# Regrouping TensorE's queue in a local-attention and channel-mix kernel: the four W_k blocks of a unit together behind the gate

## The chip, the cores and the metric

The kernel runs on one core of a Trainium2 chip. What counts is the device time of one execution in microseconds (us). Engines are named as in the profile: PE is TensorE's matmul stream and PEld its weight loads, DVE is VectorE, ACT is ScalarE, POOL is GpSimd, and SP is the engine that issues all DMAs.

## The reference

A chunked local attention feeds a channel mix. The attention works for each of 4 batches and 8 heads on chunks of 32 queries. Each chunk sees 16 keys to its left, its own 32, 8 to its right, and 8 memory keys.

```python
scores = scale * np.matmul(q_c, k_full.transpose(0, 1, 3, 2))
a = np.exp(scores - np.max(scores, axis=-1, keepdims=True))
a = a / (np.sum(a, axis=-1, keepdims=True) + 1e-09)
out[:, :, c_start:c_end] = np.matmul(a, v_full)
...
xk = mu_k * x + (1.0 - mu_k) * x_prev
xr = mu_r * x + (1.0 - mu_r) * x_prev
k = np.maximum(xk @ w_k, 0.0)
v = k * k @ w_v
r = 1.0 / (1.0 + np.exp(-(xr @ w_r)))
return (r * v).astype(np.float32)
```

Here x is the attention's output with its heads side by side (4 x 768 tokens of 512 values), x_prev is x one token earlier, w_k is 512 x 1024, w_v 1024 x 512 and w_r 512 x 512.

## The kernel before, in words

The 3072 tokens are cut into 12 units of 256 tokens (two tiles of 128). For each unit TensorE runs these pieces of work, and each is one operation of a planner:

- s (L358): the scores of one unit's two tiles, 128 small products of 64 columns;
- t (L420): per tile, four transposes of the normalised weights to PSUM tile pt. DVE and ACT copy them to aTz;
- a (L437): per tile, 32 small products of 64 columns, the attention's output px. It is copied to xT (helper lines L262 on ACT, L264 on DVE);
- g (L523): the gate x @ w_r, two blocks (pr, one for each tile of 128 tokens) of 12 products of 512 columns;
- h (L535): the hidden layer x @ w_k, four blocks h0 to h3 (ph), each 24 products of 256 columns;
- v (L549): the output k*k @ w_v, four half blocks v0 to v3 (pv: v0 and v1 fill the first tile's bank, v2 and v3 the second's) of 12 products of 512 columns.

Operands of g, h and v are split in a high and a low part (xh and xl, wkh and wkl, and so on), so that each mathematical product is three on TensorE: high x high, high x low, low x high. Each product is preceded by a weight load of its own of 128 columns.

Between h and v, each hidden block goes through relu (L624 on ACT, L626 on DVE), square (L631, L633), the high part kh and the low part kl (L641). Between a and the gate stands the mix on DVE: df (L485), the two mixes of four instructions each (L493), then the high parts xh on ACT or DVE and the low parts xl (L503). The mix for the gate has index 1 in its names (xf, xh_1, xl_1), that for W_k index 0 (written over df; xh_0, xl_0). DVE multiplies each output tile with the gate (L682), and SP stores it (L685).

The order of all engines' queues is fixed when the program is built. te_order (L177 to L196) writes a sequence of TensorE's pieces. LEAD is its start, and for each later unit the loop appends the rest: h0, h1, both t of the next unit, h2, both a of the next unit, h3, v0, the s of the unit after next, v1, the two g of the next unit, v2, v3. The place in it gives each piece a due time. Plan.order (L106 to L174) then simulates the engines. A hand-written list, FIRST (L41), goes first. After it the planner picks, of all ready operations, the one that could start earliest, with due times as the second key. TensorE's operations are picked by the same rule, so their final order is mostly that of te_order. PSUM has four banks under the tag m for h, g and v blocks, handed out in turn, so each block waits until the bank that was given out four blocks earlier has been read.

Unit 0 is a special case: its h runs with the four row tiles of w_k outside and the blocks inside, as the weights arrive.

Of the kernel before, what the change touches and what calls it, by code (L numbers as in the profile page):

```python
# [16 lines left out]
P = 128  # L17
# [7 lines left out]
KT = DM // P  # L25
# [2 lines left out]
NEG = -3.0e38  # L28
TINY = 2.0**-112
LEAD = """s0 t0 t1 a0 a1 h0.0 h0.1 s1 h0.2 h0.3 g0.0 g0.1 t2 t3 a2 a3  # L30
v0.0 v0.1 v0.2 v0.3 g1.0 g1.1 s2"""
UTOK = 256
QPU = UTOK // P
QKW = NPAIR * NJ * (CHUNK + NK)
# [28 lines left out]
class Slot:  # L63
    def __init__(self, tag):
        self.tag = tag
        self.users = []


class Op:
# [3 lines left out]
    def __init__(self, name, alts, fn, deps, new, use, due, table):  # L73
        self.name = name
        self.alts = alts
        self.table = table
        self.fn, self.new, self.due = fn, list(new), due
        self.deps = [d for d in deps if d is not None]
        for s in dict.fromkeys(list(new) + list(use)):
            s.users.append(self)  # L80


class Plan:
# [22 lines left out]
    def order(self, listed):  # L106
        self.dues()
        free, ring, left, succ = {"port": 0.0}, {}, {}, {}
        state = {"table": "exp"}
        for o in self.ops:  # L110
            o.eng = o.end = None
            left[o] = len(o.deps)
            for d in o.deps:
                succ.setdefault(d, []).append(o)
        ready = [o for o in self.ops if not left[o]]
        done = []

        def place(o, only=None):
            at = list(o.deps)
            for k, s in enumerate(o.new):  # L120
                h = ring.get(s.tag, []) + [x for x in o.new[:k] if x.tag == s.tag]
                if len(h) >= self.bufs[s.tag]:
                    at += h[-self.bufs[s.tag]].users
            at = [d for d in at if d is not o]
            if any(d.end is None for d in at):
                return None
            best = None
            for eng, cost, port in o.alts:
                if only and eng != only:
                    continue  # L130
                if eng == "act" and o.table and o.table != state["table"]:
                    cost += TABLE
                t = free.get(eng, 0.7)
                for d in at:
                    t = max(t, d.end + (SELF[eng] if d.eng == eng else HOP))
                if port:
                    t = max(t, free["port"])
                key = t + cost + BIAS.get(eng, 0.0) * (len(o.alts) > 1)
                if best is None or key < best[0] - 1e-9:
                    best = (key, t, eng, cost, port)  # L140
            return best

        def put(o, p):
            _, t, eng, cost, port = p
            o.eng, o.start = eng, t
            free[eng] = t + cost
            if port:
                free["port"] = t + cost
            if eng == "act" and o.table:
                state["table"] = o.table  # L150
            o.end = t + cost + (DLAT if eng == "dma" else 0.0)
            for s in o.new:
                ring.setdefault(s.tag, []).append(s)
            ready.remove(o)
            done.append(o)
            for x in succ.get(o, ()):
                left[x] -= 1
                if not left[x]:
                    ready.append(x)

        byname = {o.name: o for o in self.ops}
        for item in listed:
            name, _, eng = item.partition("@")
            o = byname[name]
            put(o, place(o, eng))
        while ready:
            best = None
            for o in ready:
                p = place(o)
                if p is not None and (best is None or (p[1], o.due, o.seq) < best[0]):  # L170
                    best = ((p[1], o.due, o.seq), o, p)
            put(*best[1:])
        assert len(done) == len(self.ops)
        return done  # L174


def te_order():  # L177

    nu = B * S // UTOK
    seq = LEAD.split()  # L180
    seq = [tuple([x[0]] + [int(n) for n in x[1:].split(".")]) for x in seq]
    for u in range(1, nu):
        a, b = 2 * u + 2, 2 * u + 3
        g = [("g", u + 1, c) for c in range(QPU)]
        h = [("h", u, f) for f in range(FT // 2)]
        v = [("v", u, n) for n in range(FT // 2)]
        seq += h[:2] + [("t", a), ("t", b)] + h[2:3] + [("a", a), ("a", b)] + h[3:]
        seq += v[:1] + [("s", u + 2)] + v[1:2] + g + v[2:]
    last = {"s": nu, "g": nu, "t": B * NQT, "a": B * NQT}
    seq = [x for x in seq if x[1] < last.get(x[0], nu)]  # L190
    due, t = {}, 8.0
    for x in seq:
        assert x not in due
        due[x] = t
        t += PE_COST[x[0]]
    return due  # L196
# [3 lines left out]
def local_attention__then__channel_mix(  # L200
# [11 lines left out]
    nc = tc.nc  # L212
# [57 lines left out]
    units = [(b, u * UTOK) for b in range(B) for u in range(S // UTOK)]  # L270
    NU = len(units)
    due = te_order()
    chunks = [(w_r, wr_hl, k) for k in range(KT // 2)]
    chunks += [(w_k, wk_hl, k) for k in range(KT)]
# [53 lines left out]
    def wdeps(hl, ks):  # L328
        return [o for k in ks for o in wdone[id(hl[0]), k]]
# [181 lines left out]
    def channel_mix(u):  # L511
        b, t0 = units[u]

        def hilo(m):
            return T["xh", u, m], T["xl", u, m]
# [11 lines left out]
        def hidden(f, ks):  # L527
            p = T["ph", u, f]
            xh, xl = hilo(0)
            for i in range(2):  # L530
                fc = slice((2 * f + i) * P, (2 * f + i + 1) * P)
                for k in ks:
                    wh, wl = (w[k][:, fc] for w in wk_hl)
                    for n, (w, x) in enumerate(((wh, xh), (wh, xl), (wl, xh))):
                        nc.tensor.matmul(  # L535
                            p[:, i * UTOK : (i + 1) * UTOK], w, x[:, k],
                            start=(k + n == 0 and (u > 0 or i == 0)), stop=(k == KT - 1 and n == 2 and (u > 0 or i == 1)),
                        )

        def value(c, fs):  # L540
            p = T["pv", u, c]
# [19 lines left out]
        for n in range(QPU):  # L561
            def f_gate(n=n):
# [9 lines left out]
            w = wdeps(wr_hl, [n] if first else range(KT // 2))  # L572
            prev = op(
                f"g{u}.{n}", ("pe", BLOCK), f_gate, [prev] + xg + w,
                new=(gs if n == 0 else []) if first else [gs[n]], use=xgs + gs * first, due=due["g", u, n],
# [11 lines left out]
        for c in range(QPU):  # L587
# [3 lines left out]
                    new=[sgs] if c == 0 else [], use=[gs[c], sgs], due=due["g", u, QPU - 1] + BLOCK + 2,  # L591
# [7 lines left out]
        for n in range(FT // 2):  # L599
            def f_hidden(n=n):  # L600
                if first:
                    for f in range(FT // 2):
                        if n == 0:
                            bank("ph", u, f)
                        hidden(f, [n])
                else:
                    bank("ph", u, n)
                    hidden(n, range(KT))

            w = wdeps(wk_hl, [n] if first else range(KT))  # L610
            prev = op(
                f"h{u}.{n}", ("pe", BLOCK), f_hidden, [prev] + xk + w,
                new=(ms if n == 0 else []) if first else [ms[n]], use=xks + ms * first, due=due["h", u, n],
            )
            hdone.append(prev)
# [4 lines left out]
        for f in range(FT // 2):  # L620
# [22 lines left out]
            s, kf, kh, kl = ms[f], Slot("kf"), Slot(f"kh{f}"), Slot(f"kl{f}")  # L643
# [11 lines left out]
        for n in range(FT // 2):  # L655
# [13 lines left out]
            if first:  # L669
                new, use = (vs if n == 0 else []), use + vs  # L670
            else:
                new, use = ([vs[c]] if half == 0 else []), use + [vs[c]]
# [33 lines left out]
    with tc.manual_schedule():  # L706
        for o in plan.order(FIRST.split()):
            if o.eng == "pe":
                n = 0 if ("ph", 0, 0) in T else int((o.start - busy - 0.1) / (0.86 if busy else 1.72))
# [53 lines left out]
```

## Time and profile before

| | |
|---|---|
| device time, three runs | 421.63, 423.3, 423.85 us; median 423.3 us |
| profiled execution, first to last instruction | 420.3 us |
| mean granted TensorE clock | 0.996 |
| PE busy | 407.5 us (97%) |
| PEld busy | 354.2 us (84%) |
| DVE, ACT, POOL busy | 249.1, 186.6, 19.0 us |
| DMA queue of the data (q1) | 48.31 MB, 31.4% of 16 engines' span |

The profile shows one execution, and no time of its own beside its span; the three runs are 1.3 to 3.6 us longer than that span. The duration that the profile gives a single product covers its whole way through the array and overlaps its neighbours, so the rate of TensorE is read from the distance of starts. In the chain of waits a piece counts from the end of the one before it.

### The profile page before, as it was taken

The numbers are of one execution on the slowest core, as the hardware profiler recorded it, in microseconds if no ns is written. First come the engines' busy times: TensorE is split into PE (matmuls) and PEld (weight loads), VectorE is DVE, ScalarE is ACT, GpSimd is POOL, SyncE is SP. The second block draws the span as 40 slices with busy tenths as digits, with TensorE's granted clock in tenths as the row PEclk, the third lists the DMA queues.
The fourth block names the chain that finished last, engine by engine and source line by source line (L and its number), as shares of the span: only waits on it lengthen the run. The fifth ranks groups of instructions, "written<-read, shape, count | busy, mean of one in ns | idle before, by whom it ended". The sixth has DMA issues, their size and how long they took to land.

```text
span 420.3 us, 9878 instructions
## 1 busy us (share of the span) xinstructions
PE 407.5 (97%) x4450; PEld 354.2 (84%) x4450; DVE 249.1 (59%) x357; ACT 186.6 (44%) x274; POOL 19.0 (5%) x20
## 2 busy tenths in 40 slices
PE   6988999999999999999999999999999999999996
PEld 2447989878988988988988998998998998898994
DVE  3898989990394385386276277178179069165021
ACT  2376874760543453363354354255155255153250
POOL 2202000200000000000000000000000000000000
PEclk9899999999999999999999999999999999999999
DMA  8996966210073043034034034024030010000001
GB/s 321 389 413 236 400 209 246 76 50 27 25 249 105 25 143 136 27 117 161 27 102 176 27 101 176 27 101 177 25 101 28 25 51 28 25 2 27 25 2 50
DMA packets 12905, 48.93 MB, mean 116 GB/s; under 512 B 1472, under 2 KB 1600, under 8 KB 12352
## 3 DMA queue, kind: packets, MB, share of 16 engines
q1 hardware_dynamic: 12864, 48.31, 31.4%
q8 instruction: 35, 0.57, 0.6%
q14 instruction: 6, 0.05, 0.0%
HBM read 42.01 MB, written 6.29 MB: 115 GB/s over the span
## 4 chain that ended last, share of the span: by engine, by line
PE 85%; DMA 6%; DVE 5%; ACT 2%; issue 1%; SPq 0%; DVEq 0%; ACTq 0%
PE ph L535 30%; PE pv L549 30%; PE pr L523 14%; DMA qk<-in_qk_dram 6%; PE px L437 5%; PE s L358 4%; PE pt L420 2%; DVE mag L311 1%; DVE wvl L317 1%; DVE xl L503 1%; DVE df L493 0%; DVE xh L264 0%; DVE wvh L264 0%; ACT L383 0%; DVE kl L641 0%
## 5 line engine op out<-in xcount | busy, mean ns | idle before, releaser
L535 PE MATMUL ph<-xh,wkh 128*128 128x256 f32 x384 | 109.6, 285 | 0.0
L535 PE MATMUL ph<-xh,wkl 128*128 128x256 f32 x384 | 107.8, 281 | 0.0
L535 PE MATMUL ph<-xl,wkh 128*128 128x256 f32 x384 | 107.8, 281 | 0.0
L624 ACT ACTIVATE kf<-ph 128x512 f32<-128x512 f32 x46 | 27.4, 597 | 127.6 <-PE ph L535 124.6
L549 PE MATMUL pv<-wvh,kh 128*128 128x512 f32 x192 | 75.7, 394 | 0.5 <-ACT kf L624 0.5
L549 PE MATMUL pv<-wvh,kl 128*128 128x512 f32 x192 | 74.8, 390 | 0.0
L549 PE MATMUL pv<-wvl,kh 128*128 128x512 f32 x192 | 74.8, 390 | 0.0
L535 PEld LDWEIGHTS ph<-xh,wkh 128*128 128x128 f32 x384 | 72.4, 188 | 1.1
L535 PEld LDWEIGHTS ph<-xh,wkl 128*128 128x128 f32 x384 | 73.3, 191 | 0.0
L535 PEld LDWEIGHTS ph<-xl,wkh 128*128 128x128 f32 x384 | 72.1, 188 | 0.4
L641 DVE TENSOR_TENSOR kl<-kf,kh 128x512 fp32r<-128x512 f32 x48 | 32.9, 689 | 48.1 <-ACT kh L262 47.3
L682 DVE TENSOR_TENSOR o<-pv,sg 128x512 f32<-128x512 f32 x24 | 16.4, 688 | 71.8 <-PE pv L549 71.8
L549 PEld LDWEIGHTS pv<-wvh,kh 128*128 128x128 f32 x192 | 36.0, 188 | 8.4 <-ACT kf L624 0.9
L549 PEld LDWEIGHTS pv<-wvh,kl 128*128 128x128 f32 x192 | 36.0, 188 | 7.6
L549 PEld LDWEIGHTS pv<-wvl,kh 128*128 128x128 f32 x192 | 36.1, 188 | 6.8
L523 PE MATMUL pr<-wrh,xh 128*128 128x512 f32 x96 | 37.6, 392 | 0.0
L523 PE MATMUL pr<-wrh,xl 128*128 128x512 f32 x96 | 37.4, 389 | 0.0
L523 PE MATMUL pr<-wrl,xh 128*128 128x512 f32 x96 | 37.4, 389 | 0.0
L437 PEld LDWEIGHTS px<-aTz,vw 128*64 128x64 f32 x768 | 23.6, 138 | 5.2 <-issue 3.3
L631 ACT ACTIVATE kf<-kf 128x512 f32<-128x512 f32 x39 | 24.5, 632 | 7.1 <-DVE kf L626 6.0
L262 ACT CAST kh<-kf 128x512 fp32r<-128x512 f32 x38 | 23.6, 620 | 8.4 <-PE pv L549 5.4
L437 PE MATMUL px<-aTz,vw 128*64 128x64 f32 x768 | 25.5, 224 | 1.2 <-DMA vw<-in_vw_dram 1.0
(60 smaller groups left out, 481.7 us busy)
## 6 DMA issues: line engine op xcount, KB each, us to landing
qk<-in_qk_dram SPq DMA_DIRECT2D x24, 768.0 KB, 6.4
vw<-in_vw_dram SPq DMA_DIRECT2D x24, 512.0 KB, 4.6
out_dram<-o SPq DMA_DIRECT2D x24, 256.0 KB, 2.0
raw<-in_w_k_dram SPq DMA_DIRECT2D x4, 1024.0 KB, 8.9
raw<-in_w_v_dram SPq DMA_DIRECT2D x4, 1024.0 KB, 6.4
raw<-in_w_r_dram SPq DMA_DIRECT2D x2, 1024.0 KB, 7.5
id_sb<-in_ident_dram SPq DMA_DIRECT2D x1, 64.0 KB, 7.4
mu_sb<-in_mu_dram SPq DMA_DIRECT2D x1, 4.0 KB, 7.1
```

Of the source, the lines that this page charges most:

```text
L262: e.copy(dst, src)
L311: nc.vector.scalar_tensor_tensor(mi, mi, 3, word(0, U32), ALU.logical_shift_left, ALU.bitwise_or)
L358: nc.tensor.matmul(s5[CHUNK * j : CHUNK * (j + 1), h, c, r, :], q4[z, r, j, :], k4[z, r, j, :], start=True, stop=True,)
L420: nc.tensor.transpose(p[:, n * P : (n + 1) * P], e[:, n // 2, c, n % 2, :], id_sb)
L437: nc.tensor.matmul(p3[64 * h : 64 * h + 64, 2 * g : 2 * g + 2, CHUNK * j : CHUNK * j + CHUNK], v[:, g, h, j, :], a[:, h, g, j, :], start=True,
L523: nc.tensor.matmul(p, x[:, k, c * P : (c + 1) * P], w, start=(k + n == 0), stop=(k == KT - 1 and n == 2))
L535: nc.tensor.matmul(p[:, i * UTOK : (i + 1) * UTOK], w, x[:, k], start=(k + n == 0 and (u > 0 or i == 0)), stop=(k == KT - 1 and n == 2 and ...
L549: nc.tensor.matmul(p, x[:, tc_], w, start=(f + n == 0), stop=(f == FT - 1 and n == 2))
L624: e.activation(r, T["ph", u, f], AF.Relu)
L631: e.activation(q, q, AF.Square)
L641: e.tensor_sub(l, T["kf", u, f], T["kh", u, f].bitcast(F32))
L682: nc.vector.tensor_mul(o, T["pv", u, c], T["sg", u][:, c * DM : (c + 1) * DM])
```

## The change

Four things change.

1. te_order: in units 2 to 11 the four h blocks stand together, and before them stand the two gate blocks of the same unit. The small pieces come behind them: both t of the next unit and s, then v0, both a, v1, v2, v3, and the next gate. In unit 1 the order of what is left after LEAD stays as it was.
2. Plan.order: TensorE's operations are taken strictly in te_order's sequence (LEAD now names v1.0 ahead of v0.3, where the planner had put it). For the other engines the first key is no longer the earliest start alone: up to 0.4 us (of the planner's own time) is added for operations that are due late.
3. hidden: in every unit but the first, the very first product of h0 is issued as two products of 128 columns each, with the same weights, each with a weight load of its own.
4. As a result the planner deals out some of DVE's, ACT's and POOL's work differently.

```diff
-v0.0 v0.1 v0.2 v0.3 g1.0 g1.1 s2"""
+v0.0 v0.1 v0.2 v1.0 v0.3 g1.0 g1.1 s2"""
...
+        line = sorted((o for o in self.ops if o.alts[0][0] == "pe" and o.end is None), key=lambda o: o.rank, reverse=True)
         while ready:
             best = None
+            while line and line[-1].end is not None:
+                line.pop()
             for o in ready:
+                if o.alts[0][0] == "pe" and o is not line[-1]:
+                    continue
                 p = place(o)
-                if p is not None and (best is None or (p[1], o.due, o.seq) < best[0]):
-                    best = ((p[1], o.due, o.seq), o, p)
+                k = p and (p[1] + min(0.4, max(0.0, 0.05 * (o.due - p[1]))), o.due, o.seq)
+                if p is not None and (best is None or k < best[0]):
+                    best = (k, o, p)
...
-        seq += h[:2] + [("t", a), ("t", b)] + h[2:3] + [("a", a), ("a", b)] + h[3:]
-        seq += v[:1] + [("s", u + 2)] + v[1:2] + g + v[2:]
+        x = [("a", a), ("a", b)]
+        seq += h + [("t", a), ("t", b), ("s", u + 2)]
+        seq += x + g + v[1:] if u == 1 else v[:1] + x + v[1:] + g
...
-                        nc.tensor.matmul(
-                            p[:, i * UTOK : (i + 1) * UTOK], w, x[:, k],
-                            start=(k + n == 0 and (u > 0 or i == 0)), stop=(k == KT - 1 and n == 2 and (u > 0 or i == 1)),
-                        )
+                        start = k + n == 0 and (u > 0 or i == 0)
+                        stop = k == KT - 1 and n == 2 and (u > 0 or i == 1)
+                        step = P if u > 0 and f + i + k + n == 0 else UTOK
+                        for a in range(0, UTOK, step):
+                            nc.tensor.matmul(
+                                z[:, a : a + step], w, x[:, k, a : a + step], start=start and a == 0, stop=stop
+                            )
```

The places below are those of unit 4. The numbers behind a tile's name are those that the program gave it; the changed program's lines stand up to 11 further down (L535 is L547, L485 is L492, and so on). First TensorE's queue where the unit's h begins, before (ph is the hidden block, pv the output bank of the unit before):

```order
L549 MATMUL pv_1_1914<-wvl_81,kh_3_1778 128x512
L549 MATMUL pv_1_1914<-wvh_77,kl_3_1849 128x512
L535 MATMUL ph_0_1941<-xh_0_1851,wkh_66 128x256
L535 MATMUL ph_0_1941<-xl_0_1874,wkh_66 128x256
L535 MATMUL ph_0_1941<-xh_0_1851,wkl_70 128x256
L535 MATMUL ph_0_1941<-xh_0_1851,wkh_67 128x256
```

and with the change (pr is the gate of the same unit):

```order
L530 MATMUL pr_1_1931<-wrl_85,xh_1_1885 128x512
L530 MATMUL pr_1_1931<-wrh_83,xl_1_1904 128x512
L547 MATMUL ph_0_1946<-xh_0_1906,wkh_66 128x128 x2
L547 MATMUL ph_0_1946<-xl_0_1927,wkh_66 128x256
L547 MATMUL ph_0_1946<-xh_0_1906,wkl_70 128x256
L547 MATMUL ph_0_1946<-xh_0_1906,wkh_67 128x256
```

The gate now stands directly ahead of h, and the first product is two of 128 columns. Next the place where the transposes leave the h stream, before (between h1 and h2):

```order
L535 MATMUL ph_1_1969<-xl_0_1874,wkh_69 128x256
L535 MATMUL ph_1_1969<-xh_0_1851,wkl_73 128x256
L420 MATMUL pt_2001<-id_sb,e_1889 128x128 x4
L420 MATMUL pt_2008<-id_sb,e_1889 128x128 x4
L535 MATMUL ph_2_2015<-xh_0_1851,wkh_66 128x256
L535 MATMUL ph_2_2015<-xl_0_1874,wkh_66 128x256
```

and with the change (behind h3; s is the scores tile, pv the unit's own first output bank):

```order
L547 MATMUL ph_3_2037<-xl_0_1927,wkh_69 128x256
L547 MATMUL ph_3_2037<-xh_0_1906,wkl_73 128x256
L427 MATMUL pt_2069<-id_sb,e_1804 128x128 x4
L427 MATMUL pt_2076<-id_sb,e_1804 128x128 x4
L365 MATMUL s_2083<-qk_1435 32x64 x32
L365 MATMUL s_2083<-qk_1490 32x64 x32
L560 MATMUL pv_0_2151<-wvh_74,kh_0_2001 128x512
L560 MATMUL pv_0_2151<-wvl_78,kh_0_2001 128x512
```

The small pieces have left the h stream, and transposes and scores now follow each other. Last DVE's queue between the attention's output and the operands of the next gate, before:

```order
L485 TENSOR_TENSOR df_2121<-xT_2086 128x1024
L493 SCALAR_TENSOR_TENSOR xf_2123<-df_2121,mu_sb,xT_2086 128x256 x4
L264 CAST xh_1_2144<-xf_2123 128x1024
L493 SCALAR_TENSOR_TENSOR df_2121<-df_2121,mu_sb,xT_2086 128x256 x4
L641 TENSOR_TENSOR kl_3_2217<-kf_3_2141,kh_3_2146 128x512
L503 TENSOR_TENSOR xl_1_2221<-xf_2123,xh_1_2144 128x1024
L367 MEMSET s_2152 32x2x4x16
L371 TENSOR_REDUCE mx_2238<-s_2152 128x16
L503 TENSOR_TENSOR xl_0_2242<-df_2121,xh_0_2219 128x1024
L375 TENSOR_TENSOR e_2257<-s_2152,mx_2238 128x1024
```

and with the change:

```order
L382 TENSOR_TENSOR e_2173<-s_2083,mx_2167 128x1024
L271 COPY xT_2212<-px_2177 128x4x128
L271 COPY xT_2212<-px_2195 128x4x128
L492 TENSOR_TENSOR df_2232<-xT_2212 128x1024
L500 SCALAR_TENSOR_TENSOR xf_2234<-df_2232,mu_sb,xT_2212 128x256 x4
L693 TENSOR_TENSOR o_0_2252<-pv_0_2151,sg_1944 128x512
L500 SCALAR_TENSOR_TENSOR df_2232<-df_2232,mu_sb,xT_2212 128x256 x4
L510 TENSOR_TENSOR xl_1_2273<-xf_2234,xh_1_2254 128x1024
L394 TENSOR_REDUCE sum_2277<-e_2173 128x16
L395 TENSOR_SCALAR sum_2277<-sum_2277 128x16
```

The copies of px to xT have come from ACT to DVE, the score reductions have moved ahead of them, and the cast to xh_1 has gone to ACT. POOL, which normalised one unit's weights (L393) in the lead, no longer does that; DVE does it, behind the mix.

More of the change, by code (lines that the diff above doesn't have):

```diff
@@ L76, in __init__ @@
         self.table = table
-        self.fn, self.new, self.due = fn, list(new), due
+        self.fn, self.new, self.due, self.rank = fn, list(new), due, due
         self.deps = [d for d in deps if d is not None]
@@ L531, in hidden @@
                 fc = slice((2 * f + i) * P, (2 * f + i + 1) * P)
+                z = p[:, i * UTOK : (i + 1) * UTOK]
                 for k in ks:
```

## The prediction

> **What bounds the kernel now.** I read the page first. TensorE is busy almost throughout, at full clock nearly everywhere.
>
> ```profile
> PE 407.5 (97%) x4450; PEld 354.2 (84%) x4450; DVE 249.1 (59%) x357; ACT 186.6 (44%) x274; POOL 19.0 (5%) x20
> PEclk9899999999999999999999999999999999999999
> ```
>
> As many weight loads as products: each product has its own. Next the list of waits says who kept PE idle.
>
> ```profile
> PE s L358 <- DMA qk<-in_qk_dram: 4.5, 3, 2.7
> PE s L358 <- issue: 1.7, 1, 1.7
> PE px L437 <- DMA vw<-in_vw_dram: 1.0, 1, 1.0
> PE pv L549 <- ACT kf L624: 0.5, 1, 0.5
> ```
>
> The first three lie in the lead, where this change moves nothing on TensorE. The fourth is at 85 us. The chain of waits (start, duration) then shows where the time goes.
>
> ```profile
> 38.70 11.10 PE ph L535 x96
> ...
> 80.94 2.85 DVE mag L311
> 83.79 0.02 issue
> 83.81 1.05 ACT wvh L262
> 84.86 0.50 ACT kf L624
> 85.36 0.04 issue
> 85.41 5.73 PE pv L549 x24
> 91.14 5.44 PE pr L523 x24
> ...
> 137.09 5.66 PE ph L535 x48
> 142.75 0.87 PE pt L420 x8
> 143.62 2.83 PE ph L535 x24
> 146.45 2.02 PE px L437 x64
> 148.46 3.02 PE ph L535 x24
> 151.49 2.72 PE pv L549 x12
> 154.21 1.41 PE s L358 x89
> 155.62 2.95 PE pv L549 x12
> 158.57 5.44 PE pr L523 x24
> 164.01 5.44 PE pv L549 x24
> ...
> 394.28 11.31 PE ph L535 x96
> ```
>
> From 85.41 us to the end the chain is TensorE alone, one unit in 32.36 us (137.09 to 169.45). So only three things count: how fast products follow each other, what entering and leaving a stream costs, and a new wait, if there is one. Of the 32.36 us the h stream takes 11.51.
>
> Is its rate what it could be? I asked the timeline for starts of single products, in unit 0 and in unit 3.
>
> ```profile
> 38.63 0.39 PE L535 MATMUL ph<-xh,wkh 128*128 128x256 f32 x1
> 38.85 0.28 PE L535 MATMUL ph<-xl,wkh 128*128 128x256 f32 x1
> 38.97 0.28 PE L535 MATMUL ph<-xh,wkl 128*128 128x256 f32 x1
> 39.43 0.28 PE L535 MATMUL ph<-xh,wkh 128*128 128x256 f32 x1
> 49.63 0.27 PE L420 MATMUL pt<-id_sb,e 128*128 128x128 f32 x1
> 136.93 0.28 PE L535 MATMUL ph<-xh,wkh 128*128 128x256 f32 x1
> 142.59 1.03 PE L420 MATMUL pt<-id_sb,e 128*128 128x128 f32 x8
> ```
>
> Unit 0: the start at 39.43 is its seventh product, so 90 products take 49.63 - 39.43 = 10.20 us, 113.3 ns each. Unit 3: 48 products take 142.59 - 136.93 = 5.66 us, 117.9 ns each. Same shapes, same operand buffers, same clock. The whole last unit also runs slowly (11.31/96 = 117.8). So the h stream has two cadences, each of which holds itself up: products and their loads settle into a rhythm, and which one is decided at the entry. This is the largest term of the change.
>
> **The change part by part.** *Entry of h (split and gate ahead).* What entries does the trace show? A wide product (pv, and pr ahead of unit 1) is followed at once by the slow cadence; so are the transposes and, in the units, px. Only unit 0 ended fast, and that entry looked different: the first two starts are 0.22 us apart, the next 0.12, then the distance falls to 0.113. There the second load could start only behind the first, so products and loads began in step. The split makes such an entry: a half product streams for about half of 113 ns, less than a load takes, so twice in a row a product must wait for its load and starts as the load ends. With the gate ahead it does so in the same way in all eleven units, and with the four blocks together it is needed once per unit. I take the fast cadence: 95 whole products x (117.8 - 113.3) ns x 11 units = **-4.7 us**. The bounds are 0 (cadence stays) and that. The trace has only one entry that went fast and nine px entries that didn't, so the chance is only a little over one half.
>
> The Trainium skill's page "SBUF — State Buffer", section "Who interferes with whom", says that PE reads moving operands and weights through two independent ports and never waits on anyone; by that, an entry could not matter, and the sum would be that of the first rival below. The two cadences above speak against it, 113.3 against 117.9 ns at the same clock.
>
> *Price of the split.* One product becomes two. The nearest row is the transposes: 128 columns, a load each, 0.87 us for 8, or 109 ns. Two at 109 instead of one at 113.3 is +0.105 us, x 11 = **+1.15 us**. The upper end is the first start behind px, 0.22 us, for each half: +0.33 us, +3.6 in all. Below nothing is excluded, since both halves bring a load of their own.
>
> By the Trainium skill's page "TensorE: Matmul & The Clock Gate", section "Back-to-back issue gap", 128 columns cost about 81 ns sustained; the split would then be an estimated +0.5 us and the sum 0.6 lower. The transposes' 109 ns decide.
>
> *Order of small pieces.* In the chain's rows an entry shows as the surplus of the next piece. Before, per unit: h behind t 0 (2.83), h behind px 0.19 (3.02 against 2.83), v behind s 0.23 (2.95 against 2.72), together 0.42. After: s behind t, where I take 0 since the 1.41 behind pv includes the same entry; v behind s 0.23; v behind px, not in the trace, between 0.19 and 0.23: together 0.46 at most. That is +0.04 x 8 units, **+0.3 us**. Grouping as such gains nothing.
>
> *The stall at 85 us.* The wait of 0.5 us and the refill (5.73 - 5.44 = 0.29) go back to one DVE instruction.
>
> ```profile
> 80.03 2.67 POOL L393 TENSOR_TENSOR e<-e,sum 128x1024 f32<-128x1024 f32 x1 [43.85 <-DVE sum L389]
> L371 DVE TENSOR_REDUCE mx<-s 128x16 f32<-128x1024 f32 x12 | 14.7, 1224 | 0.4
> ```
>
> The mag join took 2.85 us in the chain while POOL normalised weights; DVE work of that size takes 1.22. POOL no longer does this, so the join ends some 1.6 us earlier (one square comes to DVE ahead of it, the sums of L387 go behind), and the relu behind it frees the bank of v1.0 in time. Next late would be kl_1, now behind a mix of four L493 instructions, and it is needed only at v1.0's seventh product, 1.4 us in. I take the whole **-0.8 us**; the other end is 0.
>
> *New waits.* The pieces of the attention come later, so the mix has less time. From px's end to the next gate stand v1 (2.95), v2 and v3 (5.44): 8.39 us, where there were 3.02 + 2.72 + 1.41 + 2.95 = 10.10. What must fit is DVE's queue up to xl_1, from these rows:
>
> ```profile
> 143.88 1.30 DVE L264 COPY aTz<-pt 64x512 f32<-64x512 f32 x2 [1.28 <-ACT aTz L262]
> 149.14 1.23 DVE L485 TENSOR_TENSOR df<-xT 128x1024 f32<-128x1024 f32 x1 [0.21 <-ACT xT L262]
> 150.40 1.67 DVE L493 SCALAR_TENSOR_TENSOR xf<-df,mu_sb,xT 128x256 f32<-128x256 f32 x4
> 154.91 1.21 DVE L503 TENSOR_TENSOR xl<-xf,xh 128x1024 fp32r<-128x1024 f32 x1
> 159.76 0.68 DVE L682 TENSOR_TENSOR o<-pv,sg 128x512 f32<-128x512 f32 x1
> ```
>
> One copy of px (0.65), df 1.23, xf 1.67, the output product 0.68, the other mix 1.67, xl 1.21: 7.1 us, and 0.2 until px is visible. It fits with 1.1 us to spare, and another 0.45 because the gate's third product is the first to read xl_1. Ahead of the copies DVE has max, kl_3 and the subtraction, done before px ends, since v0 (2.95) and both a (2.02) stand between s and px's end. xl_0 comes 3.6 us behind xl_1 (sum, output product, xl itself) and has the gate's 5.44 us as cover. The cast to xh_1 on ACT runs beside the second mix. SP's queue now issues qk, then vw, then both outputs; qk and vw wait for s and px there, and what they load is read a unit later. Cost 0; if a cover goes, each late us costs one us in each of nine units.
>
> The sum: -4.7 + 1.15 + 0.3 - 0.8 = -4.05 us. The profiled span is 420.3 and would be 416.3; against the median of 423.3, which holds 3.0 us around that span, **419.3 us** (-0.95%). A measurement of this kernel can tell about 0.5%, 2.1 us, from no change.
>
> **The rivals.** *The cadence stays slow in all units*: -4.7 falls away, +0.65 remains, 423.9 us. For it: 117.8 behind every wide product, and nine px entries, which were load-bound too and ended slow. Against it: unit 0. *Some units only*: half of them gives 421.6; against it, the queue around h is the same in every unit, so they should all go one way. *Slower*: the stream settles in a third rhythm, that of the 0.12 us which the third product of unit 0 showed at first. If that holds itself up, 96 x 2.2 ns x 11 = 2.3 us on top of the slow sum: 426.2 us; it decides from about 119.2 ns on, and a split at its upper price (+3.6) gives 426.4 with the slow cadence. Against it: no stream in the trace stays there. *xl_1 late at the gate*: it decides once DVE's queue loses over 1.5 us, as the mag join did beside POOL; 1 us beyond is 9 us, 428.3; against it, POOL's only instruction of a unit, a square, is over before px ends. *Better than 113.3*: the load-bound 109 ns, another 4.5 us, 414.8; no row shows h there.
>
> **How the numbers follow.** Fast cadence in all units 0.56; better still 0.03; some units 0.08 (0.03 of it beyond 0.5%); slow cadence 0.20; third rhythm or dear split 0.08; xl_1 late 0.05. So faster 0.62, same 0.25, slower 0.13. The likeliest case alone spans 418.4 (split at half its price, no surplus of entries) to 421.7 (split at its upper price); the runs of before scatter by 2.2 us. The range must take in the slow cadence with a little scatter: 417.6 to 424.8.
>
> **What would show it.** Right: starts of h products 113 ns apart from the first dozen on in units 1 to 11, 96 in about 10.9 us; no wait of PE at the gate; no gap near 85 us; a unit in some 32.0 us. Wrong: 117.8 ns behind the split; PE waiting for L510 at the gate; the two halves more than 0.25 us together.

## The result and the profile after

The changed kernel takes 419.38 us (median of six runs, 418.10 to 419.95) against 423.18 us for the kernel before on the same chip (six runs, 421.63 to 423.85): a ratio of 0.9916, 95% interval 0.9893 to 0.9938. The prediction said 419.3. Set against the kernel before a second time on another chip, the change gave 420.09 us and 0.9929 (0.9903 to 0.9955).

On the page the two PE rows have hardly moved (97% busy, full clock), so the page cannot tell where 3.8 us went:

```profile
PE 406.5 (97%) x4461; PEld 352.3 (84%) x4461; DVE 247.1 (59%) x356; ACT 193.3 (46%) x275; POOL 17.7 (4%) x20
PEclk9898999999999999999999999999999999999999
```

All PE waits of the changed kernel lie in the lead. The row of pv behind kf has gone, and no row of pr has come, so nothing waits at the gate:

```profile
PE s L365 <- DMA qk<-in_qk_dram: 3.1, 3, 2.2
PE s L365 <- issue: 2.2, 1, 2.2
PE px L444 <- issue: 1.2, 1, 1.2
PE warm L723 <- DVE zero_sb L258: 1.1, 1, 1.1
```

The chain of waits (start, duration) shows the difference:

```profile
40.21 11.08 PE ph L547 x96
...
66.92 11.00 PE ph L547 x97
77.92 13.62 PE pv L560 x60
...
105.14 11.00 PE ph L547 x97
116.14 0.87 PE pt L427 x8
117.01 1.42 PE s L365 x89
118.43 2.94 PE pv L560 x12
121.37 2.02 PE px L444 x64
123.39 8.38 PE pv L560 x36
131.77 5.44 PE pr L530 x24
137.21 11.00 PE ph L547 x97
...
392.21 11.00 PE ph L547 x97
403.21 10.91 PE pv L560 x48
```

A unit now takes 137.21 - 105.14 = 32.07 us, where it took 32.36. The h stream is one piece of 11.00 us in all eleven units behind the first, and TensorE runs through 85 us without a gap. The start of single products in one h stream (x2 is the pair of halves):

```profile
137.05 0.33 PE L547 MATMUL ph<-xh,wkh 128*128 128x128 f32 x2
137.22 0.33 PE L547 MATMUL ph<-xl,wkh 128*128 128x256 f32 x1
...
137.51 0.28 PE L547 MATMUL ph<-xh,wkh 128*128 128x256 f32 x1
...
148.05 0.38 PE L427 MATMUL pt<-id_sb,e 128*128 128x128 f32 x2
```

The start at 137.51 is the third whole product behind the pair. From it to the transposes, 93 products take 148.05 - 137.51 = 10.54 us, 113.3 ns each. That is the shorter of the two cadences; below they are called the 113 and the 118 cadence. The granted clock was 1.00 from 60 us to 416 us in both profiles, and in those of all experiments.

How do 3.84 us in the trace, 2.3 in the spans (420.3 to 418.0) and 3.8 in the medians go together? The lead differs from execution to execution: in this profiled one unit 0's h began at 40.21, in that of before at 38.70, so 1.5 us of the gain is hidden in the two spans. About 1.3 us of these went with the granted clock: it was 0.53 from 35.1 to 38.1 us here and 1.00 in before, and four transposes and 32 products of px there took 1.04 and 1.90 us where they took 0.59 and 1.08. I therefore compare from the first h product of unit 1, which starts at

```profile
65.28 0.28 PE L535 MATMUL ph<-xh,wkh 128*128 128x256 f32 x1
```

before, and with the change at

```profile
66.76 0.33 PE L547 MATMUL ph<-xh,wkh 128*128 128x128 f32 x2
```

to the end of the last output block, which before is

```profile
405.59 10.89 PE pv L549 x48
```

The ends are 405.59 + 10.89 = 416.48 before and 403.21 + 10.91 = 414.12 after. That is 351.20 against 347.36 us, -3.84. (The changed kernel's profiled execution took 419.76 us, 1.8 more than its span.)

### The profile page after: what moved, and what is told of

Read it like the earlier page. It is cut to its first block, busy times and chain, and to the rows that moved or that the text cites. A ratio compares the mean times of both kernels' runs of the same rounds, so it can differ in the third digit from the quotient of the medians.

```text
span 418.0 us, 9919 instructions
## 1 busy us (share of the span) xinstructions
PE 406.5 (97%) x4461; PEld 352.3 (84%) x4461; DVE 247.1 (59%) x356; ACT 193.3 (46%) x275; POOL 17.7 (4%) x20
## 4 chain that ended last, share of the span: by engine, by line
PE 92%; DMA 6%; issue 1%; SPq 0%; DVE 0%
PE pv L560 32%; PE ph L547 32%; PE pr L530 16%; DMA qk<-in_qk_dram 6%; PE px L444 6%; PE s L365 4%; PE pt L427 2%; PE warm L723 0%; SPq L295 0%; DVE o L693 0%; SPq L351 0%; SPq L421 0%
## 5 line engine op out<-in xcount | busy, mean ns | idle before, releaser
L547 PE MATMUL ph<-xh,wkh 128*128 128x256 f32 (+1 forms) x395 | 106.7, 275 | 0.0
L547 PE MATMUL ph<-xl,wkh 128*128 128x256 f32 x384 | 106.6, 278 | 0.0
L547 PE MATMUL ph<-xh,wkl 128*128 128x256 f32 x384 | 106.0, 276 | 0.0
L652 DVE TENSOR_TENSOR kl<-kf,kh 128x512 fp32r<-128x512 f32 x47 | 32.3, 689 | 113.3 <-ACT kh L269 113.2
L560 PE MATMUL pv<-wvh,kh 128*128 128x512 f32 x192 | 76.7, 400 | 0.0
L547 PEld LDWEIGHTS ph<-xh,wkh 128*128 128x128 f32 x395 | 74.1, 188 | 0.9
L547 PEld LDWEIGHTS ph<-xh,wkl 128*128 128x128 f32 x384 | 72.1, 188 | 0.0
L547 PEld LDWEIGHTS ph<-xl,wkh 128*128 128x128 f32 x384 | 72.1, 188 | 0.0
L595 ACT ACTIVATE sg<-pr 128x512 f32<-128x512 f32 x24 | 14.1, 598 | 47.7 <-PE pr L530 47.7
L269 ACT CAST kh<-kf 128x512 fp32r<-128x512 f32 x46 | 28.5, 620 | 4.1 <-POOL kf L644 2.4
L269 ACT CAST xh<-xf 128x1024 fp32r<-128x1024 f32 x11 | 11.6, 1053 | 38.0 <-DVE xf L500 38.0
```

The source lines that it names most:

```text
L269: e.copy(dst, src)
L547: nc.tensor.matmul(z[:, a : a + step], w, x[:, k, a : a + step], start=start and a == 0, stop=stop)
L560: nc.tensor.matmul(p, x[:, tc_], w, start=(f + n == 0), stop=(f == FT - 1 and n == 2))
L595: nc.scalar.activation(T["sg", u][:, c * DM : (c + 1) * DM], T["pr", u, c], AF.Sigmoid)
L652: e.tensor_sub(l, T["kf", u, f], T["kh", u, f].bitcast(F32))
```

## The experiments

The theory was that of the prediction: the halves make an entry at which products wait for their loads, and this entry decides for the 113 cadence. The rivals were that the new order does it by itself, that a shift of the right size decides and not the waiting, and that the gain is the stall's or the planner's.

### Without the split

Against the changed kernel:

```diff
-                        step = P if u > 0 and f + i + k + n == 0 else UTOK
+                        step = UTOK
```

> The changed kernel with its first h product whole again; the order of the pieces stays as in the change. Entry theory (the two halves put the h stream into its fast cadence): each of the eleven h streams falls back to 117.8 ns per product and takes 11.31 us instead of 11.00, so the median is 419.4 + 11 x 0.31 = 422.8 us. Order theory (the gate ahead and the four blocks together make the stream fast, the halves only cost): the stream stays at 113.3 ns and the 0.12 us of the second half is saved, 419.4 - 1.3 = 418.1 us.

Measured: 422.43 us, ratio to before 0.9974 (0.9949 to 0.9998). In its chain an h stream takes 11.31 us, and the rest of the unit is unchanged (137.27 - 104.88 - 11.31 = 21.08 us beside h, as 32.07 - 11.00 = 21.07 with the split):

```profile
104.88 11.31 PE ph L547 x96
...
137.27 11.31 PE ph L547 x96
```

11.31/96 = 117.8 ns, and so in all eleven units. So the order does not set the cadence; the split does, and it is worth 11 x 0.31 = 3.4 us of the 3.84.

### The split alone, in the old order

The kernel before with only the diff's part on hidden.

> The kernel before with the split alone: the first product of h0 in units 1 to 11 as two of 128 columns, the order of the pieces as before (h0 behind an output block, transposes between h1 and h2, px between h2 and h3). Entry theory: h0 and h1 run at 113.3 ns, the transposes end that, h2 and h3 run at 117.8. Nine units gain 48 x 4.5 ns - 0.12 = 0.10 us, units 1 and 11, whose 96 products stand together, 0.31 us each: 423.2 - 1.5 = 421.7 us. Order theory (it needs the gate ahead): all at 117.8 ns and the halves cost 11 x 0.11, 424.4 us.

Measured: 421.16 us, ratio 0.9954 (0.9937 to 0.9971), 0.5 us less than the theory gave. The chain shows why:

```profile
105.99 5.56 PE ph L540 x49
...
112.42 2.83 PE ph L540 x24
...
117.27 3.02 PE ph L540 x24
...
138.25 5.56 PE ph L540 x49
...
144.69 2.75 PE ph L540 x24
...
149.45 2.94 PE ph L540 x24
```

h0 and h1 behind the split are at 113 as expected (5.56 against 5.66). But from unit 3 on, h2 behind the transposes and h3 behind px went faster too (2.75 against 2.83, 2.94 against 3.02), which they did in no unit of before and not in unit 2 here, although the same instructions stand ahead of them. So the order's part, one stream in place of three pieces, is smaller than I had thought, and the list of instructions ahead of a stream does not by itself fix its cadence.

### The split in the middle of a stream

```diff
-                        step = P if u > 0 and f + i + k + n == 0 else UTOK
+                        step = P if u > 0 and f == 2 and i + k + n == 0 else UTOK
```

> The changed kernel with the split moved from the first product of h0 to the first product of h2, in the middle of the h stream. Entry theory: a pair of halves sets the cadence wherever it stands, so h0 and h1 run at 117.8 ns and h2 and h3 at 113.3: per unit 11.00 + 48 x 4.5 ns = 11.22 us, 421.8 us in all. Rival (the halves work only at the change from wide products): 117.8 ns throughout and 0.11 us for the halves, 422.8 + 1.2 = 424.0 us.

Measured: 422.17 us, ratio 0.9984 (0.9966 to 1.0001), and every stream takes 11.21 us:

```profile
105.59 11.21 PE ph L547 x97
```

Of these the 48 products ahead of the pair start 117.8 ns apart and those behind it 113.3 to 113.4. A pair of halves turns a stream that already runs at 118; it need not stand at an entry.

### The old order with the new planner

Before, with the rule for the other engines' choice and TensorE's strict sequence, the latter written so that TensorE's rows are those of before one by one.

```diff
-        seq += v[:1] + [("s", u + 2)] + v[1:2] + g + v[2:]
+        seq += [("s", u + 2)] + g + v[1:] if u == 1 else v[:1] + [("s", u + 2)] + v[1:2] + g + v[2:]
...
+                if o.alts[0][0] == "pe" and o is not line[-1]:
+                    continue
...
+                k = p and (p[1] + min(0.4, max(0.0, 0.05 * (o.due - p[1]))), o.due, o.seq)
```

> The kernel before with the change's planner rules alone: TensorE taken strictly in sequence (the sequence is that of before, row for row) and the new key for the other engines; no regrouping, no split. If the stall at 85 us comes from DVE's order, as the prediction says, the gap of 0.66 us and the refill go: 423.2 - 0.8 = 422.4 us, and the h streams stay at 117.8 ns. If the stall comes from elsewhere, a gap over 0.3 us remains near 85 us and the time stays at 423.2 us.

Measured: 422.26 us, ratio 0.9994 (0.9973 to 1.0016). The time cannot tell 0.8 us from nothing here; the trace can. The stall at 85 us is gone, and the h streams are as before:

```profile
77.58 13.60 PE pv L555 x60
...
104.78 5.65 PE ph L541 x48
```

So the stall belongs to the planner's part, and the cadence does not.

### The transposes between the gate and the halves

The changed order with the transposes moved ahead of h, and with px directly behind the scores. If waiting for loads decides, narrow transposes ahead of the halves can only help.

```diff
-        seq += h + [("t", a), ("t", b), ("s", u + 2)]
-        seq += x + g + v[1:] if u == 1 else v[:1] + x + v[1:] + g
+        y = [("t", a), ("t", b)]
+        seq += h + y + [("s", u + 2)] + x + g + v[1:] if u == 1 else y + h + [("s", u + 2)] + x + v + g
```

> A version of the changed kernel meant to be faster: from unit 2 on both transposes of the next unit stand between the gate and h0, the split first product stays at the head of h0, and behind h3 the scores and both px follow each other directly, then the four output half blocks. One change from small products to wide ones per unit falls away (0.22 us each in the changed kernel's chain, nine units). Entry theory: the halves set the fast cadence behind the transposes as well; a unit takes 32.07 - 0.22 = 31.85 us and the median is 419.4 - 2.0 = 417.4 us. Rival (the halves work only behind wide products): the h streams run at 117.8 ns, 9 x 0.42 = 3.8 us more, 421.2 us.

Measured: 425.67 us, ratio 1.0062 (1.0040 to 1.0085), so both theories missed, by 8.3 and 4.5 us. Its chain shows why:

```profile
105.54 11.41 PE ph L547 x97
...
118.36 0.49 PE px L444 x11
...
149.68 1.41 PE s L365 x89
151.09 0.85 PE px L444 x24
151.94 1.42 issue
153.36 1.39 PE px L444 x40
...
251.41 1.95 PE px L444 x61
```

First, h with halves behind transposes runs at 118 (11.41 us: 96 x 117.8 ns plus the half), in nine units; behind the gate, in units 1 and 11, it runs at 113. That is as the rival had it; the split alone doesn't decide. Second, and held by neither, in five of the nine units px stops for 0.4 to 1.6 us (5.1 us together), and the chain names nothing that it waits for ("issue"). Against the change, from unit 1's h on, this makes 9 x 0.41 + 5.1 = 8.8 us, less some nine entries of 0.2 us that this order saves: 7.0, and the trace has 420.80 - 66.45 = 354.35 against 347.20, 7.15.

Where the stops fall says more than the chain does. They come behind the 11th, 24th, 36th, 48th and 61st of px's 64 products in units 2 to 6: 12 or 13 products later in each unit. The next in this row would fall behind px, and in units 7 to 10 there is no stop. So their place moves evenly through the sequence of instructions, which a buffer or a load of data would not do by itself. The page has a DMA queue of its own for instructions (q8), and in each of the five units px goes on 1.2 to 1.5 us after a packet of 16 KB on it has landed (in unit 3 it landed at 151.90, and px went on at 153.36). Both fit with instructions that come too late for such a row of small products.

### Transposes ahead, scores and px apart

The same with v0 back between the scores and px, once with the halves and once with the first product cut into 192 and 64 columns:

```diff
+        y = [("t", a), ("t", b)]
+        seq += h + y + [("s", u + 2)] + x + g + v[1:] if u == 1 else y + h + [("s", u + 2)] + v[:1] + x + v[1:] + g
...
+                        cuts = [0, 192, UTOK] if u > 0 and f + i + k + n == 0 else [0, UTOK]
+                        for a, e in zip(cuts, cuts[1:]):
```

> The transposes again between the gate and the split product, but with the output block v0 put back between the scores s and the attention's output px. Theory (the small products ran dry: 128 of s and 64 of px in a row are issued faster than their instructions arrive): with v0 between them the gaps of 0.4 to 1.6 us inside px go, 5.1 us less, while one more entry of v (0.22 us in each of nine units) is paid, so 425.7 - 5.1 + 2.0 = 422.6 us; h behind the transposes stays at 11.41 us. Rival (the gaps come from what px waits for, not from the run of small products): they stay inside px, some 425 to 428 us.

> As the run with the transposes ahead and v0 between s and px, but the first product of h is cut into 192 and 64 columns. Theory (which rhythm follows is set by a shift of 1 to 2 ns among the first products, which depends on all that stands ahead, so no cut is right by itself): no forecast of the sign; the h streams of units 2 to 10 are 11.0 or 11.4 us, all nine alike, 422.6 - 3.7 = 418.9 us or 422.6 us. Rival (the transposes as such bring the slow rhythm, whatever the cut): 11.41 us in all nine, 422.6 us.

Measured: 421.83 us with the halves, ratio 0.9982 (0.9956 to 1.0009), and 419.27 us with the cut at 192, ratio 0.9888 (0.9857 to 0.9919). With the halves:

```profile
103.91 11.41 PE ph L547 x97
...
119.69 2.01 PE px L444 x64
```

and with the cut at 192:

```profile
103.61 11.00 PE ph L547 x97
...
118.98 2.02 PE px L444 x64
...
135.72 11.00 PE ph L547 x97
```

With the halves the theory's 422.6 is met within 0.8 us. With the other cut it had left open which of 422.6 and 418.9 it would be; it is the second, within 0.4 us. px is whole again in both kernels, in every unit: the stops came with 192 small products in a row and went when twelve wide ones stood between. And behind the same transposes the halves leave h at 118 while the other cut brings it to 113, in all nine units. The rival that transposes as such bring the 118 cadence falls. This kernel is no better than the change: its unit takes 135.72 - 103.61 = 32.11 us against 32.07, and its interval overlaps the change's.

### Other cuts behind the gate

The change's order, with the first product cut elsewhere: at 192 columns, at 64, at 240.

```diff
+                        cuts = [0, 64, UTOK] if u > 0 and f + i + k + n == 0 else [0, UTOK]
+                        for a, e in zip(cuts, cuts[1:]):
```

> The changed kernel with its first h product cut into 192 and 64 columns instead of 128 and 128. Entry theory (each part streams for less time than a load takes, so products start as their loads end): 192 columns stream for about 85 ns, less than a load's 109, so the stream becomes fast, 11.00 us per unit as with halves. Rival (what matters is by how much the cut shifts products against loads, and halves happen to fit): the stream stays at 117.8 ns, about 11.42 us per unit, 4.6 us more in all.

> The changed kernel with its first h product cut into 64 and 192 columns. Entry theory: both parts are shorter than a load, the stream becomes fast, 11.00 us per unit. Rival (the shift must fit): 117.8 ns and about 11.42 us per unit, at least for one of the two uneven cuts.

> The change with the first product of h cut into 240 and 16 columns in place of 128 and 128. Theory of the first version (both parts shorter than a load): the first part takes about as long as a load, so slow, 11.3 to 11.4 us per stream, about 423.5 to 424.7 us. Rival (a shift of the first products decides; 128 and 192 columns lock, 64 does not): the longer first part is on the locking side, 11.0 us, about 419.5 us.

Measured, one run each: 419.9, 424.7 and 424.45 us. At 192 the streams take 11.00 us, at 64 and at 240 they take 11.41. The chain with 64, and then that with 240 (its first line is unit 0, which has no split):

```profile
138.49 11.41 PE ph L547 x97
```

```profile
39.98 11.51 PE ph L547 x96
67.13 11.41 PE ph L547 x97
```

With 64 columns both parts bring loads, the first is shorter than a half, and the next product starts later behind the pair's start, 0.20 us against 0.17 with halves:

```profile
138.33 0.36 PE L547 MATMUL ph<-xh,wkh 128*128 128x64 f32 x2
138.53 0.30 PE L547 MATMUL ph<-xl,wkh 128*128 128x256 f32 x1
```

By the prediction's reason that is as good an entry as the halves, and the cadence is 118. The reason falls, and the rival is left: the shift that the entry leaves has to be right. The 240 columns came out as the first theory had it, so the rival's guess that a longer first part brings the 113 cadence falls too; of the four cuts tried behind the gate, only the two in the middle do.

### The split in every second unit

```diff
-                        step = P if u > 0 and f + i + k + n == 0 else UTOK
+                        step = P if u % 2 and f + i + k + n == 0 else UTOK
```

> The change with the split only in units 1, 3, 5, 7, 9 and 11. Theory (each stream's rhythm is decided at its own entry): 11.00 us in the odd units and 11.31 us in the five even ones, so 419.4 + 5 x 0.31 = 420.9 us. Rival (once in step, TensorE stays in step across units): 11.00 us in all, or 10.9 us where no split is paid, about 419.0 us.

Measured, one run: 421.51 us. That is 0.6 us above the theory, and the chain alternates without exception:

```profile
40.43 11.10 PE ph L547 x96
...
105.37 11.31 PE ph L547 x96
...
137.75 11.00 PE ph L547 x97
...
169.83 11.31 PE ph L547 x96
```

Nothing is carried from one unit's stream to the next; each is decided behind the gate. Both cadences stand in one execution, with the same weights and buffers.

## Why the prediction was right, and where not

*The cadence.* Size and sign were right: the rate went from 117.8 to 113.3 ns in all eleven units, so 95 x 4.5 ns x 11 = 4.7 us holds. The step that failed is its reason, "twice in a row a product must wait for its load and starts as the load ends". Three runs have such an entry and stay at 118: the cut at 64 columns, and halves behind transposes, twice. Behind the gate the second half and the product after it start 57 ns after the start of their own loads, behind transposes 61 and 58 ns, so the same waits can stand ahead of either cadence. (The trace holds starts in ns; whether a load has ended by then it doesn't show.) What the trace's starts of loads and products show instead: in both cadences a load begins ahead of its product, at 113 by a steady 110 ns, at 118 by 114 or 115 ns in turn. Behind the change's halves this distance goes 119, 114, 110 and stays; behind the cut at 64, and behind transposes and halves, it goes 118, 114, 115 and stays there. The two rows part by one or two ns in the first products; that this difference decides is argued, not shown. Unit 0 shows how little it takes: the same instructions behind px took 11.10 us in the run with every second split and 11.51 with the cut at 240. Why the one row falls to 110 and the other doesn't stays open: no rule that I tried sorts all entries of all runs, and no experiment here could set that distance itself.

So the forecast of the cadence was right with luck in it: 128 columns happen to bring the 113 cadence behind the gate, and 64 would not have. A chance of 0.56, little over one half, was as much as the reason could bear. Behind the gate the same queue did give the same result in all eleven units, as was argued, and "some units only" falls. As a rule this does not hold: with the split in the old order, h2 and h3 ran at 118 in unit 2 and at 113 from unit 3 on. Nor is the entry the only place where the cadence is decided, since a pair in the middle of a stream turns it. The Trainium skill's page "SBUF — State Buffer", section "Who interferes with whom", has PE's two ports independent and never waiting; the run with every second split, 11.31 and 11.00 us in one execution for the same products, speaks against the step from there to an h rate that is free of what stands ahead of it. No run shows a port that waits.

*Price of the split.* 11.00 - 96 x 0.1133 = 0.12 us in each of eleven units, 1.3 us; predicted 0.105 and 1.15. The two halves start 60 ns apart and the next product 109 ns later, then one entry gap of 173 ns follows. The Trainium skill's page "TensorE: Matmul & The Clock Gate", section "Back-to-back issue gap", would by its 81 ns at 128 columns have given an estimated 0.5 us in all; the 1.3 us decide against it here.

*Order of small pieces.* 21.07 us of a unit lie beside h, and 32.36 - 96 x 0.1178 = 21.05 did before: +0.02 a unit, +0.2 us in all, against +0.3. The run without the split fits with grouping as such gaining nothing: 422.43 against 423.01 us, 0.6 less, which is about the stall. So the regrouping, after which the change is named, gained little by itself; most of the gain is the split's.

*The stall at 85 us.* Gone, as the chain shows (13.62 us of pv in one piece). The reason holds: with the mag join off POOL's company it takes 1.21 us in place of 2.85. From DVE's timeline, this join, and then the low part xl_1 for unit 3's gate:

```profile
81.37 1.21 DVE L318 SCALAR_TENSOR_TENSOR mag<-mag,raw 128x1024 uint32<-128x1024 uint32 x1
...
129.26 1.22 DVE L510 TENSOR_TENSOR xl<-xf,xh 128x1024 fp32r<-128x1024 f32 x1
```

The other traces go the same way: with POOL's normalisation beside it the join took 2.92 us also in the run with the split alone; in the old order with the new planner, where POOL starts this work only at 91.69 us, it took 1.23. No run changed POOL's work and nothing else. From unit 1's h to unit 2's the time fell by 1.09 us (39.30 to 38.21), of which 0.31 is the cadence: 0.78 for the stall, against 0.8.

*New waits.* None, as the list of waits shows. xl_1 is done at 129.26 + 1.22 = 130.48, and the gate starts at 131.77: 1.3 us to spare, where I had worked out 1.1.

*The sum.* -4.7 + 1.3 + 0.2 - 0.8 = -4.0 against the -3.84 of the trace and the -3.8 of the medians. In absolute time two errors cancel: the forecast put 3.0 us around a span of 416.3; the six executions of the changed kernel have 1.8 us around a median span of 417.6, because the profiled execution of before was a short one (a median execution of it, 423.18 us, has a span of 421.2 us). The third rhythm and 109 ns were seen in no run: every h stream of every run ends at 113 or at 118. A slower kernel came another way than the rival had it: by a split that leaves 118 standing and is paid for (424.7 us with the cut at 64).

## What to carry to other kernels

Where TensorE is the bound, divide the length of each long stream by its number of products: if the same shape shows two rates in one trace, cutting the slower stream's first product in two is a cheap trial, and several cuts should be tried, since the right one depends on what stands ahead of it. A gain of this kind must be read anew after every change of order, for it can be lost without any wait appearing in the profile. A long row of small products (192 here) is better broken by wide ones, as long as the entries that this adds, about 0.2 us each here, cost less than the stops.

## What the runs showed of the hardware that I had not expected

Weight load and product settle in one of two lasting rhythms at the same granted clock (1.00), 113.3 or 117.8 ns for 256 columns. The rows that lead to the one and to the other differ by a few ns: behind the gate a cut at 128 or 192 columns gives 113.3, at 64 or 240 it gives 117.8; behind transposes 192 still gives 113.3 and 128 no longer does.

192 small products in a row (128 of the scores, 64 of px) made TensorE stop for 0.4 to 1.6 us (from start to start) in five of nine units, with nothing in the profile to wait for; with twelve wide products in between it stopped in none. The stops move by 12 or 13 products from unit to unit and end 1.2 to 1.5 us after a packet of the instruction queue has landed. That the instructions run dry there is well supported by this; no run changed the instruction queue alone.
